# A new order of all steps for a gated linear attention and a feed-forward block on one core

## The chip, the core and the metric

The kernel runs on one NeuronCore of a Trainium2 chip. The core has a matrix engine (PE, whose weight loads are listed as PEld), a vector engine (DVE), a scalar engine (ACT), GpSimd (POOL) and a queue engine (SP) that here issues every transfer. Each engine works through its own instructions strictly in the order in which the program emits them and waits on semaphores for the others. The metric is the device time of the core in microseconds. Inputs and outputs lie in HBM.

## The reference

Batch 4, 8 heads, 768 tokens, head dimension 48, and then a feed-forward block of width 384, inner width 2048:

```python
mag = np.sqrt(a_re * a_re + a_im * a_im)
scale = np.minimum(mag, 0.999) / (mag + 1e-06)
a_re_n, a_im_n = (a_re * scale, a_im * scale)
for t in range(S):
    ar, ai = (a_re_n[:, :, t, :, None], a_im_n[:, :, t, :, None])
    new_re = ar * S_re - ai * S_im
    new_im = ar * S_im + ai * S_re
    kv = np.einsum('bhd,bhe->bhde', k[:, :, t], v[:, :, t])
    S_re, S_im = (new_re + kv, new_im)
    y[:, :, t] = np.einsum('bhd,bhde->bhe', q[:, :, t], S_re)
...
h = x @ w_in                      # x: y with the heads side by side
g = np.maximum(h, 0.0) + alpha * np.minimum(h, 0.0)
return (g @ w_out).astype(np.float32)
```

The weights come as 64-bit floats and are turned into 32-bit ones in the kernel.

## The kernel before

The work is cut into 40 tasks. A task is a Python generator; each of its `yield`s marks the start of a step, which emits one instruction or a few for one engine. One letter of the string `ORDER` stands for one task, and each occurrence of the letter emits the next step of that task. The order of the letters is therefore the order of the instructions in each engine's queue; it was written out ahead and nothing reorders it later.

| letters | task | steps |
|---|---|---|
| A to I | `gates`: the products of the gates of a batch's 3 chunks of 128 tokens (A: 1 chunk, B: 2) | magnitudes on ACT and DVE (L253 to L301), products inside groups of 8 (L338 and L340, on DVE; the small ones on POOL but for batch 0), decays sent out (`decs`, L323), phases finished (L426, L429) and sent out (`phs`, L431) |
| J | `loads`: q, k, phases (PP) and decays (T) of each unit | transfers |
| K, L | half rows of v (`vsc`), and v of each unit (`V`, `VL`) | transfers |
| M | the raw weights, alpha, the first token | transfers |
| N, O | the weights' conversion, 8 pieces each | three ACT steps, one on POOL (L515), two on DVE (L517, L519) |
| P to m | `unit` 0 to 23: one batch's chunk of 128 tokens, all heads | below |
| n | `loads_x`: x of each feed-forward group | transfers |
| o | `all_mlp`: the feed-forward block | below |

A unit builds its attention in levels: for half-widths 1, 2, 4, 8, 16 and 32, DVE multiplies q and k by decays in place (L661, L663, then L717 for each level), ACT copies halves aside (L740, L756), PE multiplies keys with queries ("level products", L678), and DVE or ACT masks the result (L702, L699). Then come transposes of k (L785), the products kv (L797) and the sums over v (L817) on PE, the running state on DVE (L826, L829), the state's part of y on PE (L841), four copies out of PSUM on ACT (L855) and two transfers of y to HBM (`ysc`, L860).

The feed-forward block goes by groups of 1, 1, then ten times 2, then 1 and 1 units. For each of the 16 slices f of a group there are three feature matmuls (L889), a Relu on ACT (L896) and a "PReLU step" on DVE (L898). Output matmuls of slices that are ready (L908) follow each of these rounds. Feature results take turns in two PSUM buffers, so the matmul of slice f waits for the PReLU step of slice f - 2.

All transfers stand in one queue on SP. Tiles with few buffers (`gate` has two, KQ three, PP and V one) tie a task to the end of an earlier one: task E's first step, for instance, is a memset on POOL (L249) that must wait until task C no longer needs its buffer.

```python
    def run(self, order):
        for c in order:
            next(self.tasks[self.LETTERS.index(c)], None)
...
            t = yield DMA(N / 2, ("gates", g - 2))
            if last:
                nc.gpsimd.memset(z[:, :, n - 1:n], 0.0)
```

Of the kernel before, what the change touches and what calls it, by code (L numbers as in the profile page):

```python
# [27 lines left out]


ORDER = (  # L30
    "AAAAAAAAAAAAAAAABJJJJBBAAAAAAAAMMMMMAMAAAAAAAAAAALLLBBNNBBLABLAAALABALAAAANBNABBBBANAABABBANABOOAMBB"
    "OBBOAAAAAAKMAABBBABABABABABBAKKKKAALLKAABABABAABAABNAAAAABANBABALAAABAABNBNOBBBBOOOOBONBMNBNNBBBBNNJ"
    "OBOOOOOBBPBPCBNPCBBBBPCBBBBCCJJJOBBOBBKPPPPBCBBBBBMPNJJLNNBPNNBPBPBPBCNPBNCMBMCPPPPPJPCKKKKKKKKKKKKK"
    "BKBKPBBBMBCPBNOCNBOOBPCMNCLLCCBLPPPPPPPPPPPPPPPPCCMCBCCBKCCCPJOCOCDOJOCNNJCNNNNNCDCCKKKPCPCPPPPPPPPP"
    "CCQCOKOOOCMQCCQLDDDQCCLLLLLLJLLLLLLCLCCCJDJJJJJJJCCNJQQCDNCQCQCDDQQCDCCNNQCDDQQDDQCOCODDCDCDCCCQDDOQ"
    "CQOCQQQCDDDDKOCRQQCRQQQQQQCQQQRRRRQQQQQMnQCNDMCOCOOCDDDMCQCLQCLRCCCCRCRRLLLRCRRRoKJLQOOOOCoRoCoCRRCR"
    "oQQLLLLLoooKLLQLoQQQoQCoCDCooRooQoRRDooCCCCRRRRRRRRRRoCRCoCoCoCDoRQCJJJEooRRODooooNNNNNoEDRooRoRoooo"
    "RDnLLLLooOoOoOoRODLooRoLLLLLLRLLDNRNoLSoooooooooSoRRRRRooJJSooOoooooSoSSDSNDSSSESoooooooRoSNSSoooSDo"
    "ooSSSDJSJJEJJJJJJDoooooDoooEOSSSSooooSDoooSSSSSSooDDDDDDDooETTSSSEESooooSSSSSToSSEEESSooKSSSoSToJTTT"
    "ToooToooSToooTooSLoooToULoDLLoLDTJDDDDDDJTDoToEDTDDoDLDLoDDDDDDooLLLLLoToTLTooooooooooToTTTUTTToTooT"  # L40
    "ooTLJooDTTToooDUUTTTTTToULLLLULEEEEooEoTEoEDDDDDDDDDoDDEooooooUEToooUUUoooooonoUoEooJoUoooooUEUEDTDD"
    "DoTTUUUELEJULoooLLKLLLLKoUoooooDDooDDDJoKDKKoKoooUUUUUUooooDDDTTTTTToUoooUDUUUooooUooDUEDUUUUEUEEEoo"
    "EoEoooooooEoEEUooUooJooEoooUUUUoUUoFUUoooEEEoEoEooooooooooEEoEoEVFooFoJVVooJoFoJJnooooJJJJVJVFoLLooo"
    "oooooVVVFFLoLVoooooooooEEEEEEVoooVVVEEEEEEEEEEELEEEoEJJJooFoWWoEEoEEEVooooVVooVoooWJVVVVFLoooWooLooo"
    "oWVVVVVVWVWWJVoooVFFVooooXVWLoLLLVLLoLooKVKoEEEEWEVVVVVVVVVVVKLLWEEVoKooLLLLLooLXFWLVLLVLVLVVWWWWWoE"
    "EEEELooWooooEoEoEWEEEooJEWWWWWWWWEoooooooooJJEoEJEEEoooEWWWooooWoooWWWWWWWWWXLoooooWoFFFLXoLLXXXoXXo"
    "GLLWWooJoJLLXooXoXWWWWWWooooFoFFXXXXXXFoLooooLooFoXoFoFFFFFFFJJooFooonXoXXXXXGLLLLooFFXooooooXXXXooo"
    "XoXoFYFFFooooFoooFooXoFXXXXXXXXXFFXXXXXJJoYYJoooooLJLJFFFGoooFYLGFFFFFFFFooXoooYYYYYJYoYooXoooooooLo"
    "FFFFFoZZYYYYJooJYoYYZooooooYoooooZGoYYYYYYYYoYFLZZZZZZZFooooLoYYLFFLGFLLLLFLLooooYYoZZoYYYJYYYYJJLJJ"
    "LLGoFZZZLLFLLFLLLLFLooooLFFFFFFFFFFFooZZYooFFFFYZoGGGGFoooFYYYYYYYYZZZoooFooLooooFFFFFFZJFFFZooZZZZZ"  # L50
    "FZFoooooJZooZoZZnZZZZooZZZZZJZaZZLLFFJoLooooZZZJoooFoGaooGooaoaooooGGGLLLLLLLoLLLaaaaoooooooooaJaJaJ"
    "ooooooaGaaaaaoooHoooHoaaooooooGGoooaaGaaaGGaaaGGGooGGGooboaaaKboooooJooooooaooooaHGbGaGJGbJoaaGaabbb"
    "bJoJaaaaaabaaGLLbLLLoGoLGoLLLGaaHooHJooobboGoooooobboooGHobbbHobbooooJbooGHoJoboLHGJoooGbbbGbGbbbbJb"
    "ooocooooGoooJoonbooKoKGccoKKKKKooooooLbcccGcccooooHoooocooGoLLLbGJoJobbbobHbHGHHbbbLbHbGbbbbbLbbboGG"
    "GGGHoHoHoLoooGGGGGoGcGLcoGoGooGGGoGoGoGcGcGcccccLJoJoLooLoooLooooLLLcccLLccLdocoJocGcoGcGccGoocodooc"
    "oHHHddcHcccccccHdLcGGcGKoooLLHHGGHLoHLJLLHHoHooHooHooHdcGcdcdddcHcccooodoooGoooGGGGoGLLdLLLLLoGGGodd"
    "dddoooododoooonooooGooGodGddddooGdoddoooooooGHGddHoodJodHHHoJoJJJHHHJJJooooodooooooddddddddddddddddo"
    "HJeeooooJooooeoooooeoHooHHHHHHHdoLeeeooooooeeeeoefoofoooeeeoeoeooooJJooofLoooooLLooIeeofffeJeeooKooo"
    "oLLLLLLLLLHeeeeeeeeHHHHLooHoHoHoHeHoHeHooeeeeeeeeeeeeeeeJJIJJLLoHHeeHooHHIHfKHHfHHHHHoooHoJHoHooHffJ"
    "ooHoofgIooogoooofffILoHHoofffHoofofHHogHooooLnooooLLLooLoJoLgLHKLffffffffggoLIILggggfoooofKooooKHooL"  # L60
    "HooHgHooooHoHKKoKKHoofoIfKooofffoffffffffffLfJoJoofHfffHoooooHggggggoLLLLLooooIogoogIoooooHggIIIIooo"
    "ooooLgoggLgLLLILoooogggggoooIgILoooogggggggggggggJJJoohJJhhoLLIIJoooJJoggLgoooJooohhILLLoIoInoooLoho"
    "oiiJJhJohoLLJLLLhooooIIooooooooohhohhoIooooooihIhhhoIhhhoIIoIoIhIIIooiooooooooIIIihihhhhhhhooohLILIo"
# [937 lines left out]
```

## Time and profile before

| | |
|---|---|
| median of 3 runs | 843.26 us (841.33 to 843.42) |
| the profiled execution, span | 845.2 us |
| PE busy | 699.6 us, 83% |
| DVE busy | 653.3 us, 77% |
| ACT busy | 443.3 us, 52% |
| POOL busy | 196.3 us, 23% |
| instructions | 26866 |
| HBM read and written | 100.82 MB and 35.71 MB |

The page divides the span into 40 slices and gives each engine's busy share in tenths; PEclk is the clock granted to PE. Rows of a timeline give start, length, engine, line, operation, what is written from what is read, and in brackets the idle time before and what ended it. A line such as L898 is that of the kernel. The profiled execution has no time of its own beside the span; its span is 1.9 us above the median of the runs.

### The profile page before, as it was taken

The page shows a single profiled execution, that of the slowest core. Times are in us where ns is not written, and L with a number is a line of the kernel's source. Part 1 is how long each engine was busy: PE and PEld are TensorE (multiplying, and loading weights), DVE is VectorE, ACT ScalarE, POOL GpSimd, SP SyncE. Part 2 cuts the span into 40 slices and gives each one's busy share as a digit, 9 for nine tenths or more (in the row PEclk, how much of TensorE's full clock was granted, in tenths as well). Part 3 has the DMA queues.
Part 4 walks back from the last instruction along what each step waited for, and adds up shares of the span by engine and source line. Part 5 has one row for each costly group of instructions (what it writes and reads, how often), then busy time and mean ns, then how long its engine had stood idle before and what let it go on. Part 6 is the DMA issues. An engine that isn't in the chain of part 4 may idle for free.

```text
span 845.2 us, 26866 instructions
## 1 busy us (share of the span) xinstructions
PE 699.6 (83%) x11488; PEld 529.6 (63%) x11488; DVE 653.3 (77%) x1020; ACT 443.3 (52%) x937; POOL 196.3 (23%) x293
## 2 busy tenths in 40 slices
PE   0002316688899999999999999999999999999998
PEld 0001315566777777767777777777676777777776
DVE  5999998689998999979998997687877656345212
ACT  7679686356745656665565634555444324233211
POOL 6241421126544411450115404300124000000000
PEclk9999997879999999999999999999999999999999
DMA  8496987675469677736965467747644482231100
GB/s 240 142 270 172 281 198 207 186 203 123 118 201 255 143 182 223 182 88 172 264 166 138 134 178 181 201 107 192 159 136 106 115 204 64 69 80 38 37 29 9
DMA packets 194174, 130.91 MB, mean 155 GB/s; under 512 B 74120, under 2 KB 185864, under 8 KB 194056
## 3 DMA queue, kind: packets, MB, share of 16 engines
q1 hardware_dynamic: 194056, 129.20, 59.2%
q8 instruction: 90, 1.47, 0.8%
q14 instruction: 28, 0.23, 0.1%
HBM read 100.82 MB, written 35.71 MB: 162 GB/s over the span
## 4 chain that ended last, share of the span: by engine, by line
PE 63%; DVE 17%; DMA 6%; issue 6%; ACT 5%; SPq 2%; POOL 0%; DVEq 0%; ACTq 0%; POOLq 0%
PE ps_o L908 25%; PE ps_h L889 25%; PE ps_lv L678 4%; DVE KQ L717 4%; PE ps_y L817 3%; PE ps_kv L797 2%; PE ps_y L841 2%; DVE gate L338 2%; DMA PP<-phs 2%; DMA phs<-gate 1%; DMA g_sb<-in_w_in_dram 1%; PE ps_kt L785 1%; DVE gate L426 1%; SPq L626 1%; DVE gate L340 1%
## 5 line engine op out<-in xcount | busy, mean ns | idle before, releaser
L889 PE MATMUL ps_h<-xT,w_in_sb 128*128 128x256 f32 (+1 forms) x1344 | 302.0, 356 | 2.9 <-DVE g_sb L898 1.6
L908 PE MATMUL ps_o<-w_out_sb,g_sb 128*128 128x384 f32 x768 | 295.2, 499 | 5.1 <-DVE g_sb L898 4.9
L889 PEld LDWEIGHTS ps_h<-xT,w_in_sb 128*128 128x128 f32 x1344 | 234.3, 193 | 74.1 <-issue 3.6
L898 DVE SCALAR_TENSOR_TENSOR g_sb<-g_sb,al,ps_h 128x256 f32<-128x256 f32 (+1 forms) x224 | 97.4, 437 | 115.5 <-ACT g_sb L896 115.1
L896 ACT ACTIVATE g_sb<-ps_h 128x256 f32<-128x256 f32 (+1 forms) x224 | 79.0, 353 | 204.2 <-PE ps_h L889 202.7
L908 PEld LDWEIGHTS ps_o<-w_out_sb,g_sb 128*128 128x128 f32 x768 | 138.0, 192 | 56.7 <-DVE g_sb L898 6.9
L717 DVE TENSOR_TENSOR KQ<-KQ,T 96x1024 f32<-96x1024 f32 x120 | 148.5, 1239 | 32.1 <-PE ps_lv L678 23.2
L678 PE MATMUL ps_lv<-WQ 96*32 96x32 f32 x2304 | 34.7, 204 | 79.0 <-DVE WQ L661 55.9
L678 PEld LDWEIGHTS ps_lv<-WQ 96*32 96x32 f32 x2304 | 26.6, 116 | 99.7 <-DVE WQ L661 56.1
L740 ACT COPY WQ<-KQ 96x1024 f32<-96x1024 f32 x48 | 50.0, 1041 | 27.8 <-DVE KQ L717 27.7
L338 POOL TENSOR_TENSOR gate<-gate 128x72 f32<-128x72 f32 x42 | 29.6, 704 | 125.6 <-ACT gate L368 122.8
L855 ACT COPY T<-ps_y 48x256 f32<-48x256 f32 x96 | 30.8, 364 | 51.8 <-PE ps_y L841 51.2
L338 DVE TENSOR_TENSOR gate<-gate 128x576 f32<-128x576 f32 (+5 forms) x84 | 50.0, 595 | 1.1
L515 POOL TENSOR_SCALAR top<-top 128x768 f32<-128x768 f32 x16 | 41.5, 2602 | 32.1 <-ACT top L507 32.1
L678 PE MATMUL ps_lv<-KQ,W 96*32 96x32 f32 x1536 | 25.2, 205 | 27.5 <-ACT W L756 23.2
L817 PE MATMUL ps_y<-A,VL 64*48 64x64 f32 x2304 | 42.4, 223 | 4.1 <-DMA VL<-vsc 2.5
L699 ACT ACTIVATE A<-ps_lv,columns 128x64 f32<-128x64 f32 x144 | 36.2, 336 | 17.2 <-PE ps_lv L678 17.1
L426 DVE TENSOR_TENSOR gate<-gate 128x1152 f32<-128x1152 f32 (+2 forms) x36 | 43.6, 1235 | 0.3
L756 ACT COPY W<-KQ 96x512 f32<-96x512 f32 x48 | 30.8, 642 | 23.9 <-DVE KQ L717 21.1
L817 PEld LDWEIGHTS ps_y<-A,VL 64*48 64x48 f32 x2304 | 39.8, 124 | 5.5 <-DMA VL<-vsc 2.7
L678 PEld LDWEIGHTS ps_lv<-KQ,W 96*32 96x32 f32 x1536 | 20.3, 115 | 29.6 <-ACT W L756 24.7
L785 PE MATMUL ps_kt<-ident,KQ 96*128 96x96 f32 x192 | 26.0, 260 | 15.4 <-DVE KQ L717 12.9
(106 smaller groups left out, 912.1 us busy)
## 6 DMA issues: line engine op xcount, KB each, us to landing
T<-decs SPq DMA_DIRECT2D x48, 384.0 KB
PP<-phs SPq DMA_DIRECT2D x24, 387.0 KB
KQ<-in_q_dram SPq DMA_DIRECT2D x48, 192.0 KB
decs<-gate SPq DMA_DIRECT2D x7, 1152.0 KB
phs<-gate SPq DMA_DIRECT2D x14, 576.0 KB
KQ<-in_k_dram SPq DMA_DIRECT2D x40, 192.0 KB
vsc<-in_v_dram SPq DMA_DIRECT2D x48, 144.0 KB
VL<-vsc SPq DMA_DIRECT2D x24, 288.0 KB
```

What stands on the lines that cost most here:

```text
L338: on(4 * k).tensor_tensor(out=m, in0=w[:, 1::-1].unsqueeze(2).to_broadcast([P, 2, 2, k]), in1=pairs_of(u), op=ALU.mult)
L426: TT(out=m[:, a], in0=U5[:, 1 + a], in1=turned(off3, o)[:, a].unsqueeze(1).unsqueeze(3).to_broadcast([P, L // 2, nb, 2]), op=ALU.mult)
L515: nc.gpsimd.tensor_scalar(out=top, in0=top, scalar1=F64_SMALL, scalar2=None, op0=ALU.max)
L678: nc.tensor.matmul(t[64 * i + j:64 * i + j + HC // 2, p], lhsT=keys(n, g), rhs=queries(n, g), start=True, stop=True)
L699: nc.scalar.activation(a[:, :, cols], t[:, :, at:at + name], AF.Copy, scale=s)
L717: nc.vector.tensor_tensor(out=x, in0=x if x0 is None else x0, in1=m, op=ALU.mult)
L740: nc.scalar.copy(z.rearrange("p i n t -> p i (n t)").rearrange("p i (m h) -> p m i h", h=h), bass.AP(tensor=KQ.tensor, offset=KQ.offset + ...
L817: nc.tensor.matmul(o, lhsT=Vp[h][64 * i:64 * i + 64, s, e_ * D:(e_ + 1) * D], rhs=a, start=False, stop=False)
L889: nc.tensor.matmul(p, lhsT=w_in_sb[:, f // 2, kk, f % 2 * P:(f % 2 + 1) * P], rhs=x_of[m][:, kk], start=(kk == 0), stop=(kk == NK - 1))
L896: nc.scalar.activation(gt, p, AF.Relu, scale=-1.0)
L898: nc.vector.scalar_tensor_tensor(out=gt, in0=gt, scalar=al_1[:, f:f + 1], in1=p, op0=ALU.mult, op1=ALU.add)
L908: nc.tensor.matmul(sums[0], lhsT=gt[:, c * P:(c + 1) * P], rhs=w_out_sb[:, f], start=(f == 0), stop=(f == NF - 1))
```

## The change

Only the string `ORDER` differs: 4,292 letters before and after, every letter equally often, the last hundred (the end of the feed-forward block) the same. Instructions, buffers and their numbers stay; what changes is which steps of other tasks stand between two steps of one task, in each engine's queue. The new order was chosen with the lengths of transfers, instruction fetches and the clock taken as varying.

```diff
 ORDER = (
-    "AAAAAAAAAAAAAAAABJJJJBBAAAAAAAAMMMMMAMAAAAAAAAAAALLLBBNNBBLABLAAALABALAAAANBNABBBBANAABABBANABOOAMBB"
-    "OBBOAAAAAAKMAABBBABABABABABBAKKKKAALLKAABABABAABAABNAAAAABANBABALAAABAABNBNOBBBBOOOOBONBMNBNNBBBBNNJ"
-    "OBOOOOOBBPBPCBNPCBBBBPCBBBBCCJJJOBBOBBKPPPPBCBBBBBMPNJJLNNBPNNBPBPBPBCNPBNCMBMCPPPPPJPCKKKKKKKKKKKKK"
...
+    "AABAMMAAAAAAAAAAAAAAAAAMAAAAAMABJMNAJNNABNAAAAAAAAAAAAANKJKAKBKNBAABAAAABABBJAAAALAAAAAAABAMAAAAOKAK"
+    "AOBAAABMAAABAAABBBABLLBABAOMABAKBABABBBALNBNABABAABBOBAKBNBABBNOBNBOOOABBBOBMBBBNLONNBBBBBBOBLBBBOBN"
+    "NOBBJBKJBNJBPBBBBBOBPBBPBBBPBCCBBOBKBPPPNLBMPJCKBBCPLBLKKPBMBBOPKKOKBBCBPBCBPMBCBPBLPBNCLPLCPLBPBCP"
...
     "oooooooooooooooooooooooooooooooooooooooooooooooooooooooooooooooooooooooooooooooooooooooooooo")
```

Places that the prediction speaks of, as the two strings put them: ahead of the PReLU step 14 of group 1, DVE has 374 steps before and 370 after. Between the last add of task C (L429) and the next DVE step whose POOL half stands behind task E's memset there are 4 DVE steps before and 26 after. Group 0's first feature matmul stands, before, behind unit 2's level products for half-widths 4 and 8; after, it stands ahead of unit 1's for 16 and 32 and of unit 2's first. From group 2 on, attention matmuls break into the feed-forward stream on PE at 105 places before and 99 after.

More of the change, by code (lines that the diff above doesn't have):

```diff
@@ new lines @@
+    "CLPCCCNPJJJCJONJNPCDCPPPPPPPPPPDPCPPCJMPCCPKPCPCQCQCNOCDPJCNCQCNLQCCPQJJCPCPQCDQPPNOPOCOQCOPJPCQPPPC"
+    "DOQMCQNCQDLJQJnCQLQJCQCKKKLQDDQKOLCCKoQCKNONCQLLNCRCQNQCRQCQRNQDQQKCQMQODLCLRDQCRLNRRDDCLLORCQOLCQON"
+    "ooCRCNCRLRMKOCCOCDONCJDQQMNDQCODNCRDCDRCCQNQOLCQCROCOMLRCLRMOCLODoDQJCLCCRQKRCCQCooLooLCLRQDLLLLLLCN"
+    "QoRCDRDCDCoCKCCRCRCCCoRRRDoCKRRooRQCRCoCoooCJQQQRQooDRNoDoRRRQDJCRDRoNooooJooJoooRJoDoooORDooooooLLL"
+    "LLLoooDODoDnoRDooRoOoERDRooNNRRLDoRoSRRoooNOoNooSoEooOoooNOSLOoSoNROSSoooSJDooSJJSJSLSJOooooooSSSooS"
@@ new lines @@
+    "SLSoDooELoLLSSooooooDSSLESoJSJoSSSSSooDooSSToDoooSDoSoETDEDTDoJoSSoSSJJSSEDoTSoooKJoTTooKooLDDoEoDoS"
+    "LTKTToToDoDLSoLoDoTKoEEDTDSSoTTToSDDDLDoJLSoSSSooooSoDoDDEoooDToTToooDoEoLoooLDTnooDUoDLooEooooooEDo"
+    "oEToTTDDDDDToToDJJJETJUooDoTDToooUoTTLLLEooLooooLToDUDETUTUUToETTTToUoDLDDoUDUDoUDTDoooooUooKDoKTLUo"
+    "EUTUTTTEDDDLDoEEEoDoooooJJoDoTTKKoTToooELoooEDoooooTLUUDUULoLooLooLLoooooDoUDEUooEoETEoDooDoooooEooo"
+    "LooLUUUUoEUUEoUEoLEEoooooUEUoEoUooEEooEUoooJoVUUUUJJUoJUEUVUUEoUUUUEEVJEEEFVoVooVoJoooooVVVoJUVUoooV"
@@ new lines @@
+    "oJFEoVVoJonoJooVWooVooWVVFoEFVLoooLoVEoLLLLLLVoooWLooooVoLWEEEEEEEEEEEEEEEoLooLoLoLKWoWVFJVEEVWJVVVo"
+    "VooWooVVVoooVoWoVoKWWVoVJVVWoVVWWJEVVFEEEEEVEEJEEEWWVoLWooWoLoLLLLLEWLoEEXoFEKoLooEoWWWEFWXVWWFLWVEo"
+    "LLVFLLooWVoooVVVVFJJJJEJoooWoooWEooWEWooWWWWEWEEWWEWWWEooWEWoLEXLWFoWFLoooLoXoLWoWoLoLoEoFooXXFXooFX"
+    "oooooFELWLoLJXLJLoKoXXooLooFoooFoXoooooXXXFFXoooXXoXoooFFooFFXXoXLXXYooXFXFooXWJFXoXJooXnoXXYoYoooXX"
+    "XooJJJoYFoFXFFoGXFXXFJLXXFYYFXFFXYXLXLXooGoLLLFXoooXooLJXooYoYLYFFoJJoooYoooGFoKYoFoFoooJYFFFYYZFGFo"
```

64 lines of the change are left out of this document (25 added, 39 removed).

## The prediction

> **What bounds the kernel now.** I read the page first, then a table by stage, then the waits of a stage, then the timeline of the one stage in which the vector engine pauses. The page:
>
> ```profile
> span 845.2 us, 26866 instructions
> PE 699.6 (83%) x11488; PEld 529.6 (63%) x11488; DVE 653.3 (77%) x1020; ACT 443.3 (52%) x937; POOL 196.3 (23%) x293
> PE   0002316688899999999999999999999999999998
> DVE  5999998689998999979998997687877656345212
> ```
>
> One slice is 21 us. DVE is full from the second slice on and PE from about the twelfth. In between lies the hand-over; the table by stage, with the cuts where the rows below put them (start and end, length, then busy time of PE, PEld, DVE, ACT, POOL, the granted clock, DMA share, GB/s):
>
> ```profile
> 10.00:140.00 130.00, 24.98 (x852) 20.58 (x852) 125.47 (x260) 101.28 (x149) 38.28 (x26) 0.99 0.82 226
> 140.00:180.00 40.00, 30.82 (x438) 23.99 (x427) 27.67 (x44) 17.63 (x42) 6.91 (x6) 0.76 0.59 168
> 180.00:236.00 56.00, 48.33 (x1090) 38.03 (x1089) 54.48 (x84) 38.37 (x80) 26.40 (x37) 0.97 0.56 135
> 236.00:845.20 609.20, 595.46 (x9127) 446.97 (x9125) 444.39 (x629) 279.77 (x661) 116.23 (x200) 1.00 0.55 140
> ```
>
> So DVE sets the time from 10 to 236 us: its idle time there is 4.5 us before 140, 12.3 us from 140 to 180, and 1.5 us after. From 236 on PE sets it, with 13.7 us idle in 609. The cut at 236 is the start of group 2's first feature matmul, the first one 256 columns wide:
>
> ```profile
> 235.95 1.24 PE L889 MATMUL ps_h<-xT,w_in_sb 128*128 128x256 f32 x5
> ```
>
> The time of a changed order is then the moment at which this matmul starts, plus the PE work behind it, plus what PE loses on the way. What stops DVE between 140 and 180 is in its timeline (start, length, then the idle time before it and what ended that):
>
> ```profile
> 140.50 0.38 DVE L399 TENSOR_TENSOR gate<-gate 128x126 f32<-128x126 f32 x1
> 142.58 1.22 DVE L717 TENSOR_TENSOR KQ<-KQ,T 96x1024 f32<-96x1024 f32 x1 [1.69 <-PE ps_lv L678]
> 146.99 0.35 DVE L898 SCALAR_TENSOR_TENSOR g_sb<-g_sb,al,ps_h 128x128 f32<-128x128 f32 x1 [1.45 <-ACT g_sb L896]
> 150.09 0.35 DVE L898 SCALAR_TENSOR_TENSOR g_sb<-g_sb,al,ps_h 128x128 f32<-128x128 f32 x1 [1.25 <-ACT g_sb L896]
> 158.21 1.35 DVE L429 TENSOR_TENSOR gate<-gate 128x1152 f32<-128x1152 f32 x1
> 159.48 0.75 DVE L338 TENSOR_TENSOR gate<-gate 128x576 f32<-128x576 f32 x1
> 162.13 0.35 DVE L898 SCALAR_TENSOR_TENSOR g_sb<-g_sb,al,ps_h 128x128 f32<-128x128 f32 x1 [0.66 <-ACT g_sb L896]
> 167.07 0.56 DVE L517 TENSOR_SCALAR top<-top 128x768 uint32<-128x768 uint32 x1 [4.59 <-POOL gate L249]
> 177.34 0.35 DVE L898 SCALAR_TENSOR_TENSOR g_sb<-g_sb,al,ps_h 128x128 f32<-128x128 f32 x1 [2.52 <-ACT g_sb L896]
> ```
>
> The longest pause, 4.59 us, is a queue effect. On GpSimd a memset of gate task E (L249) stands ahead of the weight step (L515) that this DVE step needs:
>
> ```profile
> 164.84 0.10 POOL L249 MEMSET gate<- 128x3 f32 x1 [27.47 <-ACT g_sb L896]
> 164.91 2.12 POOL L515 TENSOR_SCALAR top<-top 128x768 f32<-128x768 f32 x1
> ```
>
> The memset waits until gate task C has given back its buffer, that is until the phases that the add at 158.21 finished are sent: 158.21 + 1.35 = 159.56, and 5.3 us later the memset runs.
>
> **The change, part by part.** Both orders hold the same 4,292 letters, each task equally often, and the last hundred are equal. No instruction is added or removed, so all durations stay; only what stands beside what moves. I wrote both strings out as queues per engine and compared them at fixed places.
>
> *How much stands ahead.* Group 2's first matmul needs a free PSUM buffer, so DVE must have done PReLU step 14 of group 1. Ahead of that step the old order has 374 DVE steps, the new one 370. The four that move behind it are one L318 step and, of unit 4, one L826 and two L829:
>
> ```profile
> L318 DVE TENSOR_TENSOR gate<-gate 128x576 f32<-128x576 f32 x3 | 2.2, 747 | 0.0
> L826 DVE TENSOR_TENSOR St<-St,T 96x384 f32<-96x384 f32 x10 | 7.1, 705 | 0.0
> L829 DVE TENSOR_TENSOR St<-St,ps_kv 96x384 f32<-96x384 f32 x10 | 5.4, 545 | 0.6 <-PE ps_kv L797 0.4
> ```
>
> 0.75 + 0.71 + 2 x 0.55 = 2.6 us, less four times the 0.08 us by which neighbours overlap (158.21 + 1.35 is 159.56, and the next one starts at 159.48): 2.2 us earlier. The sums of longer queue stretches below are made in this way too, each step at the median of its own kind in this trace. The sets ahead of the later groups differ by two or three such steps, and DVE has 609.2 - 444.4 = 165 us of slack there, so I count nothing for them.
>
> *The memset.* In the new order the first DVE step whose GpSimd half stands behind this memset comes 26 steps after that add, 13.4 us of DVE work (eight PReLU steps at 0.35 and four L338 steps at 0.75 among them), where the old order has 4 steps. 5.3 us to the memset, 2.1 us for the weight step behind it: 7.4, hidden with 6 us to spare. If task C's phases leave later than the add by more than those 6 us, the pause is back, one for one. I take 4.6 us as gone.
>
> *The first three pauses*, 1.69, 1.45 and 1.25 us. Between unit 2's steps for half-widths 4 and 8 the old order has four short DVE steps, the new one eighteen, four of them 1.35 us long; between PReLU steps 0 and 1 of group 0 there is now 3.2 us of work instead of 0.5, between 1 and 2 now 8.2 instead of 1.5. All three are covered: 4.4 us gone.
>
> *What is new.* The PReLU steps 2 to 8 of group 0 now stand closer: 11.2 us of other DVE work between them, where it was 18.8. PE needs for the same stretch six rounds of feature and output matmuls and unit 2's transposes, kv and y matmuls. One round is 177.48 - 176.17 = 1.31 us at full clock:
>
> ```profile
> 142.39 1.65 PE L889 MATMUL ps_h<-xT,w_in_sb 128*128 128x128 f32 x6
> 158.37 1.42 PE L797 MATMUL ps_kv<-V,T 64*64 64x48 f32 x64
> 160.49 0.88 PE L817 MATMUL ps_y<-A,VL 64*48 64x64 f32 x48
> 176.17 0.83 PE L889 MATMUL ps_h<-xT,w_in_sb 128*128 128x128 f32 x6
> 177.48 0.83 PE L889 MATMUL ps_h<-xT,w_in_sb 128*128 128x128 f32 x6
> ```
>
> 6 x 1.31 = 7.9, plus 1.4, plus 2 x 0.9, plus 0.8 for the transposes (estimated from the kv row): 11.9 us. With full clock DVE would idle 0.7 us, at half clock 23.8 - 11.2 = 12.6. The table gives a granted clock of 0.76 there; 11.9 / 0.76 = 15.7, so I take 4.5 us of idle time in place of the old 0.66 + 4.59 + 2.52 = 7.8. The six matmuls at 142.39 take twice those at 176.17: the clock is read from work, not only from its record. [...]
>
> Together from 140 to 180: idle 12.3 becomes 12.3 - 4.4 - 7.8 + 4.5 = 4.6, a gain of 7.7 us.
>
> *The early part.* Group 0's first feature matmul moves on PE ahead of unit 1's last level products (it stood behind unit 2's second ones). PE works in order, so everything behind it waits for x of group 0. That transfer needs unit 0's y written and read back. From unit 0's last state step to the DVE step that would starve (unit 1, half-width 32) the new order has 17.9 us of DVE work, the old one 31.9. The chain in between: state matmuls, copies, two transfers, the level products. The nearest rows, with the slow ones of the same stretch beside them:
>
> ```profile
> 40.69 3.75 DMA phs<-gate
> 49.79 11.17 DMA g_sb<-in_w_in_dram
> 85.86 7.83 DMA phs<-gate
> 93.70 3.90 DMA PP<-phs
> 91.85 2.25 PE L841 MATMUL ps_y<-KQ,St 96*48 96x64 f32 x32
> L855 ACT COPY T<-ps_y 48x256 f32<-48x256 f32 x96 | 30.8, 364 | 51.8 <-PE ps_y L841 51.2
> ```
>
> With 3.75 and 3.90 for the transfers and about 5.5 us for the rest (2.25 of state matmuls, four copies of 0.36, and 1.8 as an estimate for issues and level products) it is 13 us, 5 to spare. With 7.83 and 11.17 it is 24.5, and DVE starves 6.6 us. It is nearest to the short pair, since only a few transfers stand just ahead; I charge 1 us, and keep 0 to 6.6.
>
> *Behind 236.* On PE, attention matmuls break into the feature and output stream in 99 places instead of 105 (198 edges instead of 210). An output matmul pair takes 0.81 behind its own stream and 0.91 behind attention, so an edge costs 0.1 us: 1.2 us less. Of PE's waits there I count nothing as gained, bounds 0 to the 7.4 of these three:
>
> ```profile
> PE ps_lv L678 <- issue: 4.1, 2, 2.2
> PE ps_y L841 <- issue: 1.7, 2, 1.1
> PE ps_h L889 <- DVE g_sb L898: 1.6, 2, 0.8
> 161.62 0.81 PE L908 MATMUL ps_o<-w_out_sb,g_sb 128*128 128x384 f32 x2
> 164.19 0.91 PE L908 MATMUL ps_o<-w_out_sb,g_sb 128*128 128x384 f32 x2
> ```
>
> 5.8 of those 7.4 us are "issue", where instruction fetches could sit. [...]
>
> The sum: 2.2 + 7.7 - 1.0 + 1.2 = 10.1 us, 845.2 - 10.1 = 835.1 us for the profiled execution. That one lies 1.9 us above the median of the runs, 843.26, so the median goes to 833.
>
> **The rivals.** *The clock eats it* (no change). If the stretch of the PReLU steps 2 to 8 runs at half clock throughout, DVE idles 12.6 there and not 4.5; 8.1 of the 10.1 us go back, and the median is about 841. For it: PE is busy 30.8 of 40 us there and still gets 0.76. Against it: the closer PE is fed, the longer it is busy, and the table shows 0.97 right behind.
>
> *PE stands behind x* (slower). The place is PE's queue around 105 us, group 0's first matmul ahead of unit 1's and 2's products. With the long pair of transfers DVE starves 6.6 us; the queue that issues all transfers can add to it, as it was held 7.7 us for two of the small ones:
>
> ```profile
> 97.91 7.69 SPq L560 DMA_DIRECT2D vsc<-in_v_dram  x2
> ```
>
> 6.6 + 7.7 = 14.3, of which 1 is charged: 845.2 - 10.1 + 13.3 = 848.4, a median of about 847. It turns the sign once x comes over 16 us later than the chain above gives, and it costs anything at all from 5 us on. For it: DMA share is 0.82 in this stage. Against: the new order has the transfers of unit 0's y issued sooner behind their copies.
>
> *Nearly all waits go* (faster still). The rest of the pause from 140 to 180 (4.6), the 1 us charged and the 7.4 behind 236 come on top: 13.0 more, 820. It speaks for it that the new order gives the attention steps more room: the PE work between unit products for half-width 8 and 16 is 6.8 us in the median unit, where it was 5.5. Against it: a wait that is gone makes PE the next to be late.
>
> *The order does nothing that counts*: the sets ahead of each PReLU step are so alike that only local pauses can move. This is the no-change case with another cause, and I put it with the first rival.
>
> **How the numbers follow.** A measurement of this kernel tells 0.3%, some 2.5 us, from no change. Forecast (830 to 840) 0.48; nearly all waits go 0.14; no change 0.13; slower 0.25, mostly the wait for x, the rest a transfer queue held elsewhere. A sixth of the no-change case still ends just faster, so faster is 0.64, same 0.11, slower 0.25. The range takes the first three cases and most of the fourth: 818 to 849.
>
> **What would show it.** Right: DVE idle of 140 to 180 under 6 us, no GpSimd memset L249 ending a DVE pause, the first matmul of 256 columns at 226 to 228 us, and about 609 us from there to the end. The clock's rival shows as PReLU steps waiting on ACT at L896 with PEclk at 0.6 or less; the slower one as PE waiting for xT around 105 us and L717 on DVE waiting for ps_lv. The prediction is wrong in its frame if the wide matmul comes early and the time behind it grows past 615 us.

## The result, and the profile after

| | before | after |
|---|---|---|
| median of 19 runs each | 842.19 us (836.66 to 851.5) | 837.4 us (833.65 to 843.7) |
| ratio | | 0.9953, 95% interval 0.993 to 0.9975 |
| span of the first profile | 845.2 us | 834.6 us |
| span of a second profile, measured later | 846.9 us | 840.1 us |

The new order is 4 to 5 us faster, where 10.1 were forecast. The two first profiles differ by 10.6 us, but a profile is one execution: the second pair differs by 6.8, and a second timing (f1 below) gave 0.9937. A run's time is some 2 us longer than the span of its profile (836.36 us for the 834.6 of after, 848.97 for the 846.9 of before). So the first profile of before stands for about 847 us, 5 above its median, and that of after for 836.4, 1 below; this makes up the gap between 10.6 and 4.8. The forecast must be held against the medians. The page after, with the lines that answer to those shown of before:

```profile
span 834.6 us, 26848 instructions
PE 695.8 (83%) x11488; PEld 527.7 (63%) x11488; DVE 651.7 (78%) x1020; ACT 438.7 (53%) x937; POOL 200.6 (24%) x293
...
PE   0001435889998999899999999999999999999998
...
DVE  5989999999997899889988988979767652644112
...
PEclk9999755899999999999999999999999999999999
```

The table by stage of the kernel after; the last cut is where group 2's first matmul of 256 columns now starts. Columns as before (start and end, length, busy time of PE, PEld, DVE, ACT, POOL, granted clock, DMA share, GB/s):

```profile
10.00:140.00 130.00, 29.57 (x920) 25.14 (x922) 124.78 (x255) 97.85 (x143) 34.82 (x23) 0.83 0.80 219
140.00:180.00 40.00, 30.30 (x510) 23.65 (x509) 38.30 (x64) 23.25 (x53) 12.28 (x8) 0.83 0.75 203
180.00:224.00 44.00, 40.36 (x938) 32.21 (x937) 42.43 (x62) 30.52 (x73) 30.00 (x38) 1.00 0.62 152
224.00:834.60 610.60, 595.58 (x9127) 446.68 (x9125) 444.72 (x634) 280.80 (x662) 115.09 (x200) 1.00 0.54 140
```

Its timeline of PE at the wide matmul, and at group 0's first one:

```profile
223.92 1.46 PE L889 MATMUL ps_h<-xT,w_in_sb 128*128 128x256 f32 x6
...
111.01 0.79 PE L889 MATMUL ps_h<-xT,w_in_sb 128*128 128x128 f32 x2 [4.91 <-DMA xT<-ysc]
```

The waits of DVE from 10 to 224 us, all that the view lists (what waited for what, us in total, times, longest):

```profile
DVE gate L338 <- ACT gate L368: 2.4, 1, 2.4
DVE gate L396 <- ACT runs L368: 1.7, 1, 1.7
DVE g_sb L898 <- ACT g_sb L896: 1.4, 2, 1.1
```

Up to the wide matmul the gain came as forecast, and in these profiles more. It starts 12.0 us earlier (235.95 to 223.92; the second profiles say 236.3 and 224.4). In DVE's terms: it was busy 207.6 of 226 us before (125.47 + 27.67 + 54.48) and 205.5 of 214 after (124.78 + 38.30 + 42.43), so 2.1 us less work and 9.9 us less idling stand ahead of the mark. From there to the end it takes 610.7 us in one profile and 615.7 in the other, where the old order took 609.2 and 610.6.

The 12 us are not the whole truth of the front. Four kernels of the experiments below (e2, e4, e6, g2) have the old letters up to group 2 and start it at 231.0, 232.9, 230.6 and 235.5 us; with the two profiles of before the mean of the old front is 233.7. The thirteen profiles that begin with the new letters have 223.9 to 226.0, mean 224.8. So the lead is 8.9 us on average. From 140 to 180 us the four idle 6.6 to 7.3 us on DVE, not 12.3: the wait behind L249 is 2.1 to 2.9 us instead of 4.6, those of L898 for L896 3.2 to 3.8 instead of 5.9.

Where that lead goes is seen by the start of each group's first feature matmul (us from the span's start, by the traces; the last column is the version found below):

| | before | before, second | after | after, second | after, task G's loads later (h2) |
|---|---|---|---|---|---|
| group 2 | 235.9 | 236.3 | 223.9 | 224.4 | 223.9 |
| group 3 | 274.1 | 275.5 | 266.3 | 265.8 | 265.5 |
| group 4 | 331.4 | 332.9 | 328.6 | 329.2 | 327.8 |
| group 5 | 394.5 | 397.0 | 392.3 | 395.6 | 390.2 |
| group 6 | 447.6 | 449.8 | 447.8 | 451.3 | 446.1 |
| group 10 | 681.3 | 683.4 | 669.4 | 675.0 | 668.5 |
| end | 845.2 | 846.9 | 834.6 | 840.1 | 833.6 |

In these pairs the new order is twelve us ahead at group 2, level at group 6, and ahead again at the end. The table cut at group 2 and group 6, first of before, then of after, then of each one's second profile:

```profile
235.90:447.60 211.70, 208.94 (x3447) 157.26 (x3446) 193.88 (x265) 121.76 (x267) 63.40 (x95) 1.00 0.74 188
447.60:845.20 397.60, 386.62 (x5681) 289.76 (x5679) 250.61 (x365) 158.09 (x395) 52.84 (x106) 1.00 0.46 115
```

```profile
223.90:447.80 223.90, 214.37 (x3680) 161.11 (x3679) 201.26 (x276) 129.01 (x276) 60.16 (x104) 0.99 0.70 182
447.80:834.60 386.80, 381.31 (x5449) 285.65 (x5447) 243.56 (x359) 151.90 (x386) 54.93 (x97) 1.00 0.45 116
```

```profile
236.30:449.80 213.50, 209.28 (x3447) 157.19 (x3446) 194.02 (x265) 121.71 (x267) 63.91 (x96) 1.00 0.73 185
```

```profile
224.40:451.30 226.90, 216.59 (x3680) 162.48 (x3679) 200.77 (x276) 129.19 (x276) 59.40 (x104) 0.98 0.71 179
```

The stretch from group 2 to 6 grew by 12.2 us (13.4 in the second pair). PE work is 5.4 (7.3) of it: 233 matmuls that the new order does there and not behind, and some at half clock. Moved work is no loss, since it is saved again behind group 6. PE's idle time is the rest: 211.70 - 208.94 = 2.8 before and 9.5 after, 4.2 and 10.3 in the second pair. Behind group 6 it is the other way: 11.0 idle us before, 5.5 after (10.4 and 7.3). The waits of PE from group 2 to 6, of before and then of after:

```profile
PE ps_lv L678 <- issue: 1.9, 1, 1.9
PE ps_lv L678 <- ACT W L756: 0.3, 1, 0.3
PE ps_y L841 <- DVE St L829: 0.3, 1, 0.3
```

```profile
PE ps_o L908 <- issue: 3.0, 1, 3.0
PE ps_y L841 <- DVE St L829: 2.2, 2, 1.5
PE ps_h L889 <- DMA xT<-ysc: 2.1, 1, 2.1
PE ps_h L889 <- issue: 1.3, 1, 1.3
```

"issue" means that the view names nothing that releases PE. What the trace has beside these waits are packets of the kind "instruction": 90 of 16,384 bytes on one queue (q8), one for every 255 of PE's 2 x 11,488 matmuls and weight loads. In the first profile after, the 3.0 us wait begins at 333.64, a packet runs from 333.8 to 335.2, and PE goes on at 336.61. The same holds everywhere: the 20 traces of this case have 78 waits by issue of 0.4 us or more behind 225 us. All 78 end 1.2 to 1.7 us behind the end of such a packet. All 78 also stand at the same place of a block of 256: the number of PE's instructions ahead of the one that waits (its semaphore instructions counted too) is 193 more than a multiple of 256. Of the 120 other waits of PE one stands there, and it is the odd one of k1 below. So the waits by issue stand a multiple of 256 of PE's instructions apart, each behind a packet. Below, a block is the 256 instructions from one such place to the next; what PE waits for there no view names, and that it waits for what such a packet brings is my reading of these counts. A pause can cost more than its own length. This is the wait for x of group 3 in the timeline of after, 2.12 us; six matmuls of 256 columns take 2.91 us right behind it, and 1.46 at full clock:

```profile
262.09 1.46 PE L889 MATMUL ps_h<-xT,w_in_sb 128*128 128x256 f32 x6
...
266.31 2.91 PE L889 MATMUL ps_h<-xT,w_in_sb 128*128 128x256 f32 x6 [2.12 <-DMA xT<-ysc]
```

The clock's record shows half speed for 3.4 us there, from 266.4 us on: some 1.7 us of PE's work lost, half of the stretch, as an estimate.

### The profile page after: what moved, and what is told of

Same layout as the page of the kernel before. It is cut to its first block, busy times and chain, and to the rows that moved or that the text cites. A ratio compares the mean times of both kernels' runs of the same rounds, so it can differ in the third digit from the quotient of the medians.

```text
span 834.6 us, 26848 instructions
## 1 busy us (share of the span) xinstructions
PE 695.8 (83%) x11488; PEld 527.7 (63%) x11488; DVE 651.7 (78%) x1020; ACT 438.7 (53%) x937; POOL 200.6 (24%) x293
## 4 chain that ended last, share of the span: by engine, by line
PE 53%; DVE 23%; DMA 12%; POOL 4%; issue 4%; ACT 4%; SPq 1%; DVEq 0%; ACTq 0%; POOLq 0%
PE ps_o L908 22%; PE ps_h L889 20%; DVE KQ L717 4%; DMA T<-decs 4%; PE ps_lv L678 4%; DVE gate L426 3%; DVE gate L338 2%; PE ps_y L817 2%; DMA phs<-gate 2%; PE ps_y L841 2%; PE ps_kv L797 2%; DVE gate L429 2%; DMA g_sb<-in_w_out_dram 1%; POOL gate L338 1%; DVE gate L340 1%
## 5 line engine op out<-in xcount | busy, mean ns | idle before, releaser
L889 PE MATMUL ps_h<-xT,w_in_sb 128*128 128x256 f32 (+1 forms) x1344 | 297.3, 355 | 9.0 <-DMA xT<-ysc 7.0
L898 DVE SCALAR_TENSOR_TENSOR g_sb<-g_sb,al,ps_h 128x256 f32<-128x256 f32 (+1 forms) x224 | 97.5, 436 | 117.9 <-ACT g_sb L896 117.6
L896 ACT ACTIVATE g_sb<-ps_h 128x256 f32<-128x256 f32 (+1 forms) x224 | 78.8, 352 | 200.7 <-PE ps_h L889 199.4
L338 POOL TENSOR_TENSOR gate<-gate 128x72 f32<-128x72 f32 x42 | 25.8, 615 | 134.3 <-ACT gate L368 131.5
L817 PE MATMUL ps_y<-A,VL 64*48 64x64 f32 x2304 | 42.0, 224 | 4.4 <-issue 3.8
L817 PEld LDWEIGHTS ps_y<-A,VL 64*48 64x48 f32 x2304 | 39.7, 125 | 5.4 <-issue 4.5
L702 DVE TENSOR_TENSOR A<-ps_lv,mask 128x256 f32<-128x256 f32 x96 | 37.6, 412 | 0.0
L717 DVE TENSOR_TENSOR KQ<-WQ,T 96x1024 f32<-96x1024 f32 x24 | 29.5, 1231 | 6.4 <-DMA T<-decs 4.2
```

The lines of the kernel that those rows point to most:

```text
L338: on(4 * k).tensor_tensor(out=m, in0=w[:, 1::-1].unsqueeze(2).to_broadcast([P, 2, 2, k]), in1=pairs_of(u), op=ALU.mult)
L717: nc.vector.tensor_tensor(out=x, in0=x if x0 is None else x0, in1=m, op=ALU.mult)
L817: nc.tensor.matmul(o, lhsT=Vp[h][64 * i:64 * i + 64, s, e_ * D:(e_ + 1) * D], rhs=a, start=False, stop=False)
L889: nc.tensor.matmul(p, lhsT=w_in_sb[:, f // 2, kk, f % 2 * P:(f % 2 + 1) * P], rhs=x_of[m][:, kk], start=(kk == 0), stop=(kk == NK - 1))
L896: nc.scalar.activation(gt, p, AF.Relu, scale=-1.0)
L898: nc.vector.scalar_tensor_tensor(out=gt, in0=gt, scalar=al_1[:, f:f + 1], in1=p, op0=ALU.mult, op1=ALU.add)
```

## The experiments

Ratios are to the kernel before on the same chip, with 95% intervals. "New" and "old" are the two orders. Steps are named in short: h2.0.0 is the first feature matmul of group 2's slice 0, o3.0.15 the output step of group 3's first unit for slice 15, out3.0 that unit's output; "ld9 q0" is a load of q for unit 9, "G re" the load of the gates' real part for task G, "u15 y0" one of unit 15's products.

**Which stretch of the order brings what: four cuts.** Each takes one order's letters up to a step, and then the letters that are left in the other's sequence.

```diff
-ORDER = old
+ORDER = new[:step("h2.0.0")] + rest(old)     # e1: group 2's first feature matmul
+ORDER = old[:step("h2.0.0")] + rest(new)     # e2
+ORDER = new[:step("h6.0.0")] + rest(old)     # e3: group 6's
+ORDER = old[:step("h6.0.0")] + rest(new)     # e4
```

> New order up to the first feature matmul of group 2, the old order from there on. In the profiles of the two kernels that matmul came 12.0 us earlier in the new one (223.9 against 235.9 us), and at group 6 nothing of it was left (447.8 against 447.6). Theory L, the new order's own queue places between groups 2 and 6 lose it: here the matmul of group 2 comes at about 224 and the lead is kept, group 6 at 436 to 440, ratio 0.986 to 0.990. Rival U, the units cannot come faster after that in whatever order, the lead is given back to the units' chain: group 2 at about 224, group 6 at 445 to 448, ratio 0.997 to 1.000.

> Old order up to the first feature matmul of group 2, the new order from there on. Theory L: group 2 at about 236, and the new order then loses some 8 to 10 us up to group 6 (455 to 458), ratio 1.002 to 1.010. Rival U: nothing was ahead, so nothing is given back: group 6 at 448 to 450, and what the new order saves behind that shows alone, ratio 0.992 to 0.998.

> New order up to the first feature matmul of group 6, the old order from there on. Both theories: group 6 at about 448. Theory R, the gain that is left at the end is made behind group 6, by fewer pauses of PE (1.7 us of pauses over 0.15 us in the new profile, 7.4 in the old): without that part the ratio is 0.998 to 1.002. Rival: the gain left at the end is the front's after all and the two profiles only differ by chance at group 6: ratio 0.992 to 0.996, as the whole new order has.

> Old order up to the first feature matmul of group 6, the new order from there on. Theory R: group 6 at about 448, then a faster rest, ratio 0.990 to 0.996. Rival (the gain comes from the front): ratio 0.999 to 1.002.

| | ratio | group 2 at | group 6 at |
|---|---|---|---|
| e1, new to group 2, then old | 0.9956 (0.9929 to 0.9983) | 225.5 | 444.5 |
| e2, old to group 2, then new | 1.0036 (1.0009 to 1.0064) | 231.0 | 459.3 |
| e3, new to group 6, then old | 1.0016 (0.9986 to 1.0046) | 224.9 | 453.2 |
| e4, old to group 6, then new | 0.9965 (0.9939 to 0.9992) | 232.9 | 454.3 |

The front alone is worth 3.7 us at the end (e1, of 846), though its wide matmul comes 10.4 us earlier than in before's profile. The new order up to group 6 is worth nothing (e3), and the part behind group 6 alone brings 3.0 us (e4). So a part of what was measured comes from a stretch for which I had counted next to nothing, and more than half of what I had counted is gone at the end. The new order from group 2 to 6 is what costs: with the rest alike, e3 takes 5.9 us more than e1 (849.1 and 843.2) and e2 6.3 more than e4 (850.0 and 843.7). That was theory L of e1 and e2; e1 itself fell between its two theories.

The last column can't be read across for e4. Where its two parts join, the 233 matmuls follow that the new order has ahead of group 6 and the old one behind; right there PE waits 2.9 us for v of a unit (VL), and the clock is at half for 6.8 us.

**The three parts put together.** New, old from group 2 to group 6, new.

```diff
-ORDER = old
+ORDER = (new[:step("h2.0.0")] + rest(old))[:step("h6.0.0")] + rest(new)
```

> New order up to group 2's first feature matmul, old order from there to group 6's first, new order behind. If the three parts add up (new front -0.45%, new middle +0.65%, new late part -0.4%, from the four cuts before), this one has both gains and not the loss: 0.991 of the kernel before, some 7.5 us faster, and faster than the whole new order at 0.995. If the loss in the middle is only the front's lead running dry, whatever order stands there, it comes out at the new order's 0.995 or above.

0.9952 (0.9924 to 0.9979), no better than the whole new order, where 0.991 was expected if the parts add up. But this kernel has the same join as e4: of the 9.9 us that PE idles from group 2 to group 6, 3.2 stand right behind it (2.4 for VL), and the clock is at half for 10.2 us there. So it does not tell whether the parts add up.

**Is the lead spent on the wait for x of group 3?**

```diff
         for m, n in enumerate(sizes):
-            t = yield DMA(197 * n, *[("y", u) for u in range(NU) if group_of[u][0] == m], takes=(R["xT"],))
+            r = 2 if m == 3 else m
+            t = yield DMA(197 * n, *[("y", u) for u in range(NU) if group_of[u][0] == r], takes=(R["xT"],))
...
-            nc.sync.dma_start(x_of[m], ysc_of.pop(m).rearrange("(k p) s -> p k s", p=P))
+            nc.sync.dma_start(x_of[m], ysc_of[r].rearrange("(k p) s -> p k s", p=P))
```

with the new order, and the fourth letter n moved ahead of unit 4's first y transfer.

> New order, but x of group 3 is read from group 2's y (the output of group 3 is then not the reference's), and its transfer is issued right before unit 4's y is written, some 25 us earlier. It takes away the dependence of group 3 on unit 5. Theory D (the lead of 12 us at group 2 is lost because PE runs through group 2 and then waits for vector work of unit 5): the 2.1 us wait and the half clock behind it (1.7 us) go, group 3 starts some 4 us earlier, and the time falls by 3 to 5 us to 0.990 of the kernel before. Rival (the lead is lost at fetches and later waits whatever x does): group 3 starts earlier, but group 6 does not, and the time stays at 0.995.

The new order unchanged ran beside it, for a second profile, and the kernel before gave one too:

> The new order unchanged, for a second profile and for times on the same chip as the next two. The pauses of PE that are the order's own should stand at the same instruction again: the wait for x of group 3 (2.1 us), the y state products of unit 10 (1.5). Those of instruction fetches may stand at another dense run than in the first profile, with about the same sum (4.3 us between group 2 and group 6). Time 0.995 of the kernel before.

> The kernel before, unchanged, for a second profile. If its first profile stood for it, group 2's first wide matmul starts at 236 us again, within 2 us, and the time behind is 609 us within 2. If the first profile was a long one, the difference to its 842 median (5 us by the span) shows as a place: either ahead of 236 us or behind it.

f4 gave 0.9908 (0.9875 to 0.9941), f1 0.9937 (0.991 to 0.9965). The wait at group 3 is gone, but group 3 starts at 265.3 and not 4 us earlier, and group 6 at 450.3. In f1 that wait is 0.6 us without the edit, and the two groups start at 265.8 and 451.3. Whether it is worth 1 us or 2 can't be told from these intervals; the theory of 3 to 5 fell. f3's first expectation held: group 2 at 236.3, 610.6 us behind it.

**Task G's loads.** Around the 3 us wait, SP issues two loads of 574.5 KB (the gates of task G). I moved them behind it, and the task's first ACT step a little. The kernel ran three times.

```diff
-G re (326 us)  ...  G im (331 us)  ...  o3.0.15  out3.0  h4.1.0  ...  G x (342 us)  ...  G c (345 us)
+               ...                 ...  o3.0.15  out3.0  G re  G im  h4.1.0  ...  G x  G c
```

> New order, with the two loads of gate task G (574 KB each, issued at 326 and 331.5 us) moved behind the place of the 2.97 us pause, to about 337 us, and the task's first ACT step a little later. Theory B: the pause at 333.6 falls under 1.5 us, the time from 0.995 to 0.993. Theory T: it stays at 2 us or more, and the time stays within 0.2% of 0.995.

> The new order with task G's two loads later, once more, since six runs gave 0.989 with a wide interval. If the gain over the new order is real, it stays 0.3% or more below the run beside it; if it was the draw of six runs, the two agree within 0.2%. By its trace only the pause at 333.6 us (2.97 us) can have gone, so I expect 0.2 to 0.3% at most.

> New order with task G's loads later, unchanged, as the neighbour of the run before: 0.987 to 0.991 of the kernel before, with PE pauses of 8 to 10 us from group 2 to group 6, one of them 2.4 us or more at 282 or at 297 us.

0.9886 (0.9836 to 0.9935), 0.9885 (0.985 to 0.992) and 0.9904 (0.9869 to 0.994); the new order had 0.9937 beside the second. Three letters, some 4 us (I had allowed 0.3% at most): this is the best version, 836.5 to 837.6 us where the kernel before had 845.2 to 846.4. The third run's other expectation missed: PE idles 7.7 us from group 2 to group 6, and its wait at 282 us is 1.9. The pause at its place, the timeline of PE in f1 and then in f2:

```profile
334.26 0.91 PE L908 MATMUL ps_o<-w_out_sb,g_sb 128*128 128x384 f32 x2
338.42 0.81 PE L908 MATMUL ps_o<-w_out_sb,g_sb 128*128 128x384 f32 x2 [3.25 <-issue]
```

```profile
335.36 0.91 PE L908 MATMUL ps_o<-w_out_sb,g_sb 128*128 128x384 f32 x2
337.47 0.81 PE L908 MATMUL ps_o<-w_out_sb,g_sb 128*128 128x384 f32 x2 [1.20 <-issue]
```

And what the DMA engines did just before, from 330 to 336 us, f1 and then f2 (queue, kind: packets, MB, share of the 16 engines):

```profile
q1 hardware_dynamic: 1781, 2.12, 107.9%
```

```profile
q1 hardware_dynamic: 1507, 1.63, 87.9%
q8 instruction: 2, 0.03, 2.3%
```

With the loads in front the engines are full (107.9% against 87.9%), and the packet ahead of the wait's end comes later: in f1 none runs in these 6 us, without the loads two do. With the loads, the wait before this matmul, o3.0.15, was 2.97, 2.32, 3.52, 3.25 and 2.40 us (after, e2, e3, f1, f4); with the loads moved 0.69, 1.20 and 1.33 (e8, f2, h2), and 0.60 and 0.50 in h1 and g1 below. The packet behind which the wait ends starts 3.0 to 4.5 us after PE has begun the block of 256 before it in the first five, and 1.2 to 2.0 us after it in the other five. PE is through that block in 2.7 to 3.0 us at full clock. Behind the wait of e2, e3 and f1 the clock's record is at half for 3.4 us, another 1.7; behind none of the five with the loads moved. From f1 to f2 that is 2.05 us of waiting and 1.7 of clock, most of the 4 us; it is the one cause that is shown.

**Or is it the density of small matmuls?** The same waits stand behind runs of 160 to 230 small attention matmuls, which go fast: 164 of them, with their weight loads, from 278.75 to 281.38 us in the first profile after. Breaks of wide matmuls were put into such runs: three in the old order (e6), two in the new one (e7), two in the new one with G's loads later (g1), everywhere in the old one (g2), and everywhere from unit 6 to 9 in the new one with G's loads later (k1). The edit of e6, for example:

```diff
-u15 kv  u15 y0  u15 y1  u15 y2  u15 y3  ...  u15 ys  ...  relu7.7  pre7.7  o6.1.12  o6.1.13
+u15 kv  u15 y0  u15 y1  relu7.7  pre7.7  o6.1.12  o6.1.13  u15 y2  u15 y3  ...  u15 ys
```

> Old order, with wide matmuls of the feed-forward stream put into three runs of about 200 small attention matmuls (unit 9's, 15's and 19's y products): three h4.9 matmuls, o6.1.12-13 and o8.1.14-15. Each run ends in a PE pause that nothing in the trace releases (1.95, 1.25 and 2.18 us, 5.4 in all), with an instruction packet starting beside it. Theory T (a run of small matmuls is used up faster than its instructions are fetched): the three pauses fall to under 1.5 us together, the time to 0.995 to 0.997. Theory B (fetches are late because bulk transfers fill the DMA engines): these three pauses stay, 1.000. Theory F (the place in the program counts, not the density): they stay or move to the next instruction, 1.000.

> New order, with o2.1.4-5 put into the run of 228 small matmuls ahead of the pause of 1.32 us at 284 us, and o3.0.14-15 into the one of 144 ahead of the pause of 2.97 at 333.6 us. Theory T: both pauses together fall from 4.3 to about 1.5 us, the time from 0.995 of the kernel before to 0.992. Theory B: the one at 333.6 stays at 2.5 or more, since the DMA engines are full from 322 to 336 us as before. Theory F: both stay, 0.995.

> New order with task G's loads later (0.9885 twice) and with two wide output matmuls put into each of the two dense runs of unit 6 and unit 7 (228 and 196 small matmuls), where one or the other pause of 2.3 to 3.8 us stood in every profile so far (at 282 or 299 us). Density theory: neither pause is above 1 us, no half clock follows, group 4 starts 3 to 5 us earlier, and the time falls to 0.983 to 0.985. Transfer theory: the DMA engines are as full as before around 275 to 281 and 297 to 305 us, so a pause of 2 us or more stays at one of the two, and the time stays at 0.9885.

> Old order with two steps of the feed-forward stream pulled into every run of more than 100 small matmuls behind group 2's first matmul; no transfer is moved by itself. Density theory: PE's pauses behind 236 us, 9.9 and 11.0 us in the two profiles of the old order, fall under 4 us. Transfer theory: they stay at 8 or more, elsewhere. The breaks cost on their own: 286 edges between attention and stream instead of 210, by the price of the prediction (0.1 us each) 7.6 us, so by the density theory the time is about that of the kernel before, by the other 0.9% longer.

> New order with task G's loads later, and with two steps of the feed-forward stream pulled into every run of more than 100 small matmuls from unit 6's to unit 9's y products (8 breaks, 214 edges instead of 198). Race theory (PE waits when a dense run is used up before the next instructions have come): no wait by issue above 0.5 us from group 2 to group 6, where the same order without breaks had 2.7 to 4.4 us (and 4.1 at one place in its first profile); the breaks cost 16 edges at 0.16 us, 2.6 us; the time is 0.985 to 0.990 of the kernel before, the same as without breaks within 0.3%. Rival (instructions come late wherever transfers fill the DMA engines, dense or not): a wait by issue of 2 us or more stays, and the time is 0.992 or more.

In e6 the three pauses fell from 5.4 (4.8 in the second profile of before) to 1.9 us (0.47, which DVE ends, 1.45 and none) and the ratio was 0.996 (0.9923 to 0.9996): as density says. In e7, 0.9938 (0.9903 to 0.9974), the pauses at 284 and 334 fell from 4.3 to 1.4, but one of 3.85 came up at 300 us, where the first profile after had none. g1, 0.9939 (0.9905 to 0.9974), kept it with 3.85, and its break stood behind the product in which it begins. In g2 no wait by issue is left behind group 2 (7.0 and 6.9 us in the two profiles of before); its first waits of PE:

```profile
PE ps_lv L678 <- ACT W L756: 4.3, 5, 1.7
PE ps_o L908 <- ACT top L918: 3.8, 2, 2.2
PE ps_lv L678 <- DVE KQ L717: 1.1, 1, 1.1
```

My number for that run, under 4 us of pauses in all, missed: other waits took their place and the sum stayed at 10.2. Its ratio is 1.0147 (1.0094 to 1.02), since breaks cost more than I had priced them. PE is busy 608.5 us behind group 2, and 595.6 and 596.0 before:

```profile
235.50:858.60 623.10, 608.47 (x9127) 445.58 (x9125) 445.77 (x629) 279.73 (x661) 116.73 (x200) 1.00 0.54 136
```

12.5 to 12.9 us for 76 edges are 0.16 to 0.17 us each, not 0.1 (0.14 if a stretch of 3.4 us at half clock, 1.7, is taken off). And k1 spoke against density: 1.000 (0.9969 to 1.0032), with both pauses there in spite of the breaks, at 284 and 303 us. It is some 9 us above the same order without breaks, where its 16 edges were priced at 2.6; its trace has 4 to 5 us more PE work than e8 and h2, and the rest is not explained. So the gain of G's loads is shown for this order and does not survive every other change of it (g1 has 0.9939, k1 1.000). Its waits from group 2 to 6:

```profile
PE ps_y L841 <- DVE St L829: 2.7, 2, 1.6
PE ps_lv L678 <- issue: 2.6, 1, 2.6
PE ps_y L817 <- DMA KQ<-in_k_dram: 2.4, 1, 2.4
```

The third line names a transfer of k, which L817 doesn't read; an instruction packet runs from 303.0 to 304.2 beside it, PE goes on 1.5 us later, and it stands at the border of a block like the 78 waits. I count it with the waits by issue.

**Transfers at the other pause.** With G's loads later, three loads of unit 9 were moved some 10 us later too, behind group 2's last output:

```diff
-ld8 T1  ld9 q0  ld9 k0  ld9 q1  ...  out2.1
+ld8 T1  ...  out2.1  ld9 q0  ld9 k0  ld9 q1
```

> New order with task G's loads later, and three loads of unit 9 (q and k, first of their halves) moved from about 295 us to behind group 2's last output, some 10 us. They are issued just as PE reaches unit 7's y products, where its pause of 2.4 to 3.9 us stood in four of six profiles with this stretch, with an instruction packet starting in it. Transfer theory: the pause at 296 to 299 us falls under 1.5 us, and the time goes 0.2 to 0.5% below the run beside it. Rival (the fetch is due there and late whatever the transfers do): a pause of 2 us or more stays within unit 7's products, and the two times agree within 0.2%.

0.9922 (0.9887 to 0.9957), its neighbour h2 0.9904: the same. Neither trace has the pause at 297 us; both have one at 282 (1.44 and 1.90). So nothing can be told of that place. In after, f1, e8, f2 and h2, with equal letters up to there, a pause of 0.9 to 3.8 us stands at 281 to 284 us, at 296 to 299, or at both. These are two borders of blocks, two blocks apart; what decides at which of them PE waits is open.

**The front by one letter.** In the old order, task E's first step (with the memset) stands behind POOL's weight step.

```diff
-g4 re  ...  win6 max  win6 shl
+       ...  win6 max  g4 re  win6 shl
```

> Old order with one letter moved: the first step of gate task E, with its GpSimd memset, stands behind GpSimd's first weight step of weight 6 instead of ahead of it. By the prediction's term the pause of 4.59 us at 167 us goes, and group 2's first matmul comes 4 to 4.6 us earlier, at 231 to 232 us; if the pause only passes to the next wait for PE, under 2 us earlier. The end: if a lead at group 2 is kept, 0.995; if it is lost behind, as in the cut at group 2, 0.998 to 1.000.

0.9946 (0.9916 to 0.9976). Group 2 starts at 229.7, 6.2 us earlier than in the first profile of before, and from 140 to 180 DVE now idles 2.9 us instead of 12.3:

```profile
140.00:180.00 40.00, 33.32 (x641) 25.82 (x634) 37.06 (x60) 21.40 (x48) 7.08 (x6) 0.91 0.62 171
```

By the ratio one letter gives as much as the whole new order. Not all of the 6.2 us is the letter's: the mean of the old front is 233.7, so some 4 us are, and e6 starts group 2 at 230.6 with the pause in place. But no L249 ends a wait of DVE any more, and DVE idles 2.9 us where the five other kernels with this front idle 6.6 to 12.3. The pause was part of what the stretch waited for, as the prediction read it.

## Why the prediction was right, and where it failed

*What stands ahead of group 2.* Right: 2.2 us less DVE work was forecast and 2.1 came. *The memset and the three pauses.* Right: no L249 ends a wait of DVE any more, and its idle time of 140 to 180 us is 1.7 us (under 6 was the sign; 4.6 the number). *The closer PReLU steps.* Too dear: I charged 4.5 us, and 1.1 us was the longest wait for L896 in the whole front. *x of group 0.* The transfer came 4.9 us late for PE at 111 us, and DVE didn't starve, so the 1 us charged was not needed. The sum to the mark was 8.9 us, and 12.0 and 11.9 came in the two pairs of profiles. That the mean lead over all profiles is 8.9 too is luck: the terms were read from an execution with long pauses, 12.3 us from 140 to 180 where other kernels with the same letters have 6.6 to 7.3.

*The clock's rival.* Wrong. The clock was at 0.83 in two stages, by its record at half from 96 to 150 us, and DVE stayed busy (124.8 of 130 us and 38.3 of 40). In the second profile it was at half for 17 us, and group 2 started within 0.5 us of the first: in these two executions it cost the front nothing. In the old order clock and waits do go together: the two profiles with 0.76 from 140 to 180 us wait 5.9 us for L896 there, the four with 0.85 to 0.91 wait 3.2 to 3.8; which of the two is the cause is not shown. *The slower rival.* Its place did wait, with 4.9 us, under the point from which it decides.

*Behind 236.* This is the step that failed. I wrote "DVE has 609.2 - 444.4 = 165 us of slack there, so I count nothing for them", counted PE's waits at nothing, and added the front's lead to a time behind it that was to fall by 1.2 us. It grew by 1.5 and 5.1 us in the two pairs, and by the medians some 4 of the 8.9 us are lost there. Slack and waits were averages over a stage with two halves. The rows that show it are those of the first 94 us behind the mark and the last 395, before:

```profile
236.00:330.00 94.00, 93.90 (x1506) 71.41 (x1505) 88.33 (x119) 53.11 (x122) 33.36 (x40) 1.00 0.80 201
...
450.00:845.20 395.20, 384.22 (x5669) 287.83 (x5667) 248.63 (x362) 156.93 (x392) 50.59 (x104) 1.00 0.46 115
```

DVE idles 5.7 us in the 94, and 146.6 of the last 395; DMA share is 0.80 there and 0.46 at the end. Whoever starts group 2 earlier runs into a stretch in which DVE and the transfers are nearly full too, and PE's waits up to group 6 went from 2.8 to 9.5 us (4.2 to 10.3). What was added, by the views: 2.4 (3.3) us of waits by issue, 1.9 (2.4) for the state on DVE (L829), and 2.1 (0.6) for x of group 3. The largest part is shown by an experiment, the block behind task G's loads; that the full DVE causes the second is argued from the rows. The term was to be charged with some 6 to 7 us of waits and 1.7 for each drop of the clock, and credited with the 5.5 us (3.1) of idle time that the new order saves behind group 6. My bound for PE's waits, 0 to 7.4 gained, left out a loss.

*The edges.* The term of 1.2 us was mis-sized: at 0.14 to 0.17 us, 12 edges are 1.7 to 2.0 us. It does not show in PE's busy time behind the mark, 595.5 us before and 595.6 after, where 3.4 us at half clock (1.7) came on top. *The waits by issue.* I counted nothing for them, neither gain nor loss. They were up to 3.5 us at the place ahead of o3.0.15, and 4.8 to 7.1 us in all behind group 2 in the four profiles of before and after.

*The frame.* "About 609 us from there to the end" was to be wrong past 615: 610.7 and 615.7 were measured. I also set the span of a profile beside a median of times: like with like, the first profile of before lay some 4 us above its three runs, not 1.9. A part of that stands ahead of group 2, where the same letters started it up to 5.7 us sooner in other kernels; what makes these fronts differ stays open. So does what brings a wait by issue where no bulk load stands beside it (e6 and g2 speak for dense runs, k1 against).

## What to carry to other kernels

Before a lead is carried to the end of a program, ask the table by stage for the first tenth of what lies behind it: a stage's mean slack says nothing of the stretch into which the lead arrives. A wait by "issue" on the bottleneck engine is worth a look at the instruction queue's packets and at what fills the DMA engines just then; moving two bulk loads by a few letters gave another 4 us, about as much as rewriting 4,292 letters had. And measure a lead over several profiles: fronts with the same letters ended 5.7 us apart. A pause with one named releaser (a memset in the wrong place of a queue) is worth trying by itself first: one letter gave 0.9946.

## What the runs showed of the hardware

PE's waits by issue of 0.4 us or more, behind 225 us, stand a multiple of 256 of its instructions apart: all 78 in 20 traces do, and they end 1.2 to 1.7 us behind the end of an instruction packet of 16,384 bytes. Such a wait at one place of PE's program came back in five of five profiles, at 2.3 to 3.5 us, and shrank to 0.5 to 1.3 in five others when 1.15 MB of loads were moved away from it. A pause of 2.12 us on PE was followed by 3.4 us at half clock (after, at 266 us), some 1.7 us more; behind pauses of 1.95 and 2.18 us in the first profile of before the record stays at full. A break between small and wide matmuls cost 0.14 to 0.17 us an edge, measured over 76 of them in one trace; the 16 of k1 came dearer. And half clock for 54.6 us instead of 17.1, in a stretch bound by DVE, cost nothing in the two executions compared (group 2 at 223.9 and 224.4 us).
